# Another beginning, another pick of VectorE scores and of probability tiles in a two-branch attention kernel on one core

## The chip, the cores and the metric

One core of a Trainium2 chip runs the whole program. Its engines work side by side, each through its own queue in order: TensorE (PE; its weight loads are listed as PEld), VectorE (DVE), ScalarE (ACT), GpSimd (POOL) and SyncE (SP). An instruction may wait for semaphores that other engines or transfers raise; what stands behind it in its queue then waits too. The metric is the device time of one execution in microseconds, the median of several runs.

## The reference

Two attention branches over the same x (2048 x 512, 32 heads of 16), mixed by a gate for each row.

```python
x = A_x
g = sigmoid((x * gate_w).sum(-1, keepdims=True))
# branch A: 32 query heads, one key and one value head for all of them
q = (x @ wq).reshape(B, S, H, Dh).transpose(0, 2, 1, 3); k = x @ wk; v = x @ wv
p = softmax(einsum("bhqd,bkd->bhqk", q, k) * Dh ** -0.5)
a = einsum("bhqk,bkd->bhqd", p, v) ... @ wo
# branch B: 32 heads, each with its own keys and values
qkv = (x @ wqkv).reshape(B, S, 3, H, Dh) ...
b = softmax(q @ k.T * Dh ** -0.5) @ v ... @ wo
return g * a + (1 - g) * b
```

That is 2 x 32 x 2048 x 2048 exponentials, and two small matrix products around each.

## The kernel before

*Units of work.* The scores are computed with keys on the partitions and queries along the free axis. One *score* is a tile of 128 x 1024 (two heads, 512 queries each) in PSUM: eight matmuls of 32 columns by 512 (`products`, L576). There are 2048 scores, in pairs (a *quad* of two tiles `q`, `q+1`); 32 quads make a *phase*, four phases a pair of branch and head group; branch A and B alternate over four groups (`phases`, `quads`). A score becomes probabilities by one exp on ScalarE (L583), which writes a probability tile `prob0` to `prob5`. Some scores go to VectorE instead: TensorE writes them to a spare PSUM bank (`pair<-Q..`), and VectorE computes the exponential by a chain of seven passes (`chain`, L763 to L775) in tiles `vec`. The probabilities are multiplied with the values into a PSUM bank that gathers over the phase (`values`, L624), a quad at a time: in one piece of 512 columns, or in two halves of 256. TensorE takes four instructions for each of its f32 matmuls, so a full product of a quad is 32 instructions and two halves are 64; a score is 16.

*What surrounds it.* Query, key and value projections (L195) run through the other bank of `pair`, VectorE splits their result into a high and a low f16 half (L401, L404), and transfers lay the halves at the places where the score matmuls read them (`lay`, L359, issued by SP and POOL). After each phase the sums are normalised (`normalised`, L516 to L532) and multiplied by the output weights (`o_unit`).

*What sets the order.* Nothing is scheduled at run time. While the program is built, a planner (`_Plan`, `pe_step`) keeps a clock for each engine, with fixed costs (EXP 904 ns, SCORES 215, HALF 430 and so on), and writes out each engine's instructions in the order in which it believes they become possible. `score_time` says when the next score may go; until `limit` (the last exp's start plus SLACK) `pe_step` fills TensorE with value products (`value_job`), and with projection or output jobs or a VectorE score (`spare_job`). `pick` chooses the VectorE score: the last one left of the running phase, or, when the time left doesn't do for a chain, the last one of the next phase. For the next phase it asks first that the operands are laid (`laid`); for the running one it doesn't ask.

*The beginning* is written by hand up to the loop at the end of `_fast`: eight x tiles are turned by TensorE (L272; `x_in` and `x_unit`), scaled and split by ScalarE (L280) and VectorE (L285); the first query projection, the first half of the shared keys and values (`kv_products`, L300, and `kv_split`), the turn of the keys (`k_turn`, L332) and its copy (`k_put`, L335). x tile 7 and the second half of keys, values and gate (`kv_unit`, `gates`; z in L942 to L956) go through the planner as jobs.

*Probability tiles* are taken from a queue: the one that has been free longest (`free_probs.popleft()` in `score`).

## Time and profile before

| | |
|---|---|
| median of 3 runs | 1883.47 us (1883.21 to 1886.42) |
| profiled execution, its own time | 1883.59 us |
| its span, first to last instruction | 1881.8 us |
| mean TensorE clock granted | 0.990 |
| busy: PE / PEld / DVE / ACT / POOL | 94% / 45% / 65% / 96% / 20% |
| exps on ScalarE (L583) | 1942, busy 1787.0 us |
| chains on VectorE (first pass, L763) | 106 |

How to read the rows below. In a timeline row stand the start from the span's first instruction, the length, engine, line, operation, out<-in, shapes, the count of instructions that were merged, and in brackets the engine's idle time before and what ended it. In a row of stretches stand from:to, the length, then busy time and count, the clock granted to TensorE, the DMA share and GB/s. In a row of the chain of waits stand the start, the length and the work; "issue" is time in which the engine waited for nothing that the profile shows. A busy TensorE isn't TensorE at its peak, since matmuls are pipelined and their ends are modelled.

### The profile page before, as it was taken

The page shows a single profiled execution, that of the slowest core. Times are in us where ns is not written, and L with a number is a line of the kernel's source. Part 1 is how long each engine was busy: PE and PEld are TensorE (multiplying, and loading weights), DVE is VectorE, ACT ScalarE, POOL GpSimd, SP SyncE. Part 2 cuts the span into 40 slices and gives each one's busy share as a digit, 9 for nine tenths or more (in the row PEclk, how much of TensorE's full clock was granted, in tenths as well). Part 3 has the DMA queues.
Part 4 walks back from the last instruction along what each step waited for, and adds up shares of the span by engine and source line. Part 5 has one row for each costly group of instructions (what it writes and reads, how often), then busy time and mean ns, then how long its engine had stood idle before and what let it go on. Part 6 is the DMA issues. An engine that isn't in the chain of part 4 may idle for free.

```text
span 1881.8 us, 97974 instructions
## 1 busy us (share of the span) xinstructions
PE 1761.2 (94%) x45072; PEld 849.9 (45%) x45072; DVE 1217.6 (65%) x1380; ACT 1797.6 (96%) x1957; POOL 380.8 (20%) x569
## 2 busy tenths in 40 slices
PE   7999999999999999999999999999999999998994
PEld 5444444444444444444444444444444444444441
DVE  5267522969566565878558663797856856478983
ACT  4899999999999999999999999999999999999993
POOL 4302101232032111314021401231202310130000
PEclk9999999999999999999999999999999999999997
DMA  5121211223141141414133313241413213234011
GB/s 149 43 52 43 70 43 49 75 59 65 32 88 42 37 76 36 87 26 83 30 68 56 66 36 51 56 82 42 76 28 68 54 37 64 49 61 123 26 48 59
DMA packets 74067, 109.71 MB, mean 58 GB/s; under 512 B 20640, under 2 KB 29088, under 8 KB 73648
## 3 DMA queue, kind: packets, MB, share of 16 engines
q0 software_dynamic: 27808, 44.30, 14.0%
q1 hardware_dynamic: 43888, 56.41, 11.8%
q8 instruction: 355, 5.82, 1.3%
q10 hardware_dynamic: 1952, 2.66, 0.4%
q14 instruction: 64, 0.52, 0.1%
HBM read 14.75 MB, written 33.55 MB: 26 GB/s over the span
## 4 chain that ended last, share of the span: by engine, by line
ACT 67%; PE 16%; issue 12%; DVE 3%; DMA 1%; SPq 1%; POOL 0%; ACTq 0%; DVEq 0%; POOLq 0%
ACT prob L583 67%; PE pair L624 7%; PE sc L576 4%; PE pair L195 3%; DVE vec L775 1%; PE pt L272 1%; DMA K<-lokb 0%; SPq L516 0%; SPq L359 0%; DVE xT L470 0%; DVE sum L476 0%; PE pair L272 0%; DMA oT<-raw 0%; DMA vec<-in_A_x_dram 0%; PE pair L300 0%
## 5 line engine op out<-in xcount | busy, mean ns | idle before, releaser
L583 ACT ACTIVATE prob<-sc 128x1024 f32<-128x1024 f32 x1942 | 1787.0, 1077 | 23.9 <-PE sc L576 22.4
L624 PE MATMUL pair<-prob,vA 64*32 64x512 f32 (+1 forms) x8112 | 524.8, 577 | 0.1
L624 PE MATMUL pair<-prob,vB 64*32 64x512 f32 (+1 forms) x7984 | 517.4, 574 | 1.6 <-issue 1.4
L576 PE MATMUL sc<-Qb,K 64*32 64x512 f16 x7696 | 408.4, 382 | 44.7 <-ACT prob L583 36.2
L576 PE MATMUL sc<-Qa,kA 64*32 64x512 f16 x7840 | 407.7, 380 | 29.1 <-ACT prob L583 22.1
L576 PEld LDWEIGHTS <-K 64*32 64x32 f16 x8192 | 203.3, 90 | 434.0 <-issue 396.0
L576 PEld LDWEIGHTS <-kA 64*32 64x32 f16 x8192 | 202.7, 89 | 408.4 <-issue 366.9
L775 DVE SCALAR_TENSOR_TENSOR vec<-vec,vec 128x1024 f32<-128x1024 f32 x318 | 385.7, 1225 | 2.1
L763 DVE TENSOR_SCALAR vec<-pair 128x1024 int32<-128x1024 f32 x106 | 128.7, 1214 | 75.2 <-PE pair L576 74.9
L624 PEld LDWEIGHTS pair<-prob,vB 64*32 64x32 f32 x7984 | 156.5, 105 | 23.7 <-issue 4.2
L624 PEld LDWEIGHTS pair<-prob,vA 64*32 64x32 f32 x8112 | 155.2, 105 | 20.0 <-issue 2.0
L486 POOL DMA_DIRECT2D out_dram<-sum x48 | 59.4, 1240 | 384.6 <-DVE sum L476 384.6
L775 DVE SCALAR_TENSOR_TENSOR vec<-vec 128x1024 f32<-128x1024 f32 x106 | 128.8, 1215 | 0.9
L476 DVE TENSOR_SCALAR sum<-pair,gate_up 128x512 f32<-128x512 f32 x112 | 78.3, 738 | 75.1 <-PE pair L195 75.1
L523 DVE RECIPROCAL dT<-dT 128x256 f32<-128x256 f32 (+1 forms) x66 | 111.5, 1693 | 20.3 <-DMA dT<-raw 20.3
L359 POOL DMA_DIRECT2D Qa<-loqa x122 | 59.5, 495 | 294.2 <-DVE loqa L404 238.7
L359 POOL DMA_DIRECT2D Qb<-loqb x128 | 65.4, 519 | 236.2 <-PE sc L576 235.5
L401 DVE TENSOR_SCALAR hivb<-pair 128x1024 f16<-128x1024 f32 x8 | 9.8, 1224 | 122.4 <-PE pair L195 122.4
L677 DVE COPY raw<-pair 128x1024 f32<-128x1024 f32 x32 | 39.1, 1223 | 73.9 <-PE pair L624 73.7
L359 POOL DMA_DIRECT2D K<-hikb x64 | 33.3, 520 | 253.8 <-DVE hikb L401 253.8
L401 DVE TENSOR_SCALAR hikb<-pair 128x1024 f16<-128x1024 f32 x8 | 9.8, 1224 | 114.9 <-PE pair L195 114.9
L195 PE MATMUL pair<-w16ob,o 64*32 64x512 f16 x1536 | 64.4, 391 | 14.5 <-ACT o L529 6.8
(141 smaller groups left out, 1275.3 us busy)
## 6 DMA issues: line engine op xcount, KB each, us to landing
out_dram<-sum POOLq DMA_DIRECT2D x48, 512.0 KB, 5.9
dT<-raw SPq DMA_DIRECT2D x126, 64.0 KB, 2.1
vB<-vB SPq DMA_DIRECT2D x16, 384.0 KB, 4.0
Qb<-loqb POOLq DMA_DIRECT2D x128, 32.0 KB, 2.6
Qb<-hiqb SPq DMA_DIRECT2D x128, 32.0 KB, 2.5
out_dram<-sum SPq DMA_DIRECT2D x8, 512.0 KB, 3.7
xT<-out_dram SPq DMA_DIRECT2D x16, 256.0 KB, 6.9
oT<-raw SPq DMA_DIRECT2D x126, 32.0 KB, 2.9
```

The costliest lines, as they stand in the source:

```text
L195: nc.tensor.matmul(outs[n : n + COLS, i], lhs[i][rows(i), n : n + COLS], rhs[i][rows(i)], start=start, stop=stop)
L359: fns.append(lambda q=queues[(8 * p + n) % len(queues)], dst=dst, src=hilo[part][at]: q.dma_start(dst, src))
L401: nc.vector.tensor_scalar(hilo[0], pair[1], UP ** -1, None, op0=ALU.mult)
L476: nc.vector.tensor_scalar(state["sum"][:, e], pair[1][:, e], g, None, op0=ALU.mult)
L486: done = plan.on_pool([lambda: nc.gpsimd.dma_start(dst, state["sum"], accum_op=ALU.add)], t, 1300)
L523: nc.vector.reciprocal(d[:, c : c + cut], d[:, c : c + cut])
L576: nc.tensor.matmul(bank[a : a + COLS, hh], k[rows(hh), key : key + COLS], Q[src, gi, half, p][rows(hh), j * BLK : (j + 1) * BLK], start=Tr ...
L583: nc.scalar.activation(probs[u], sc, AF.Exp, scale=SCALE / (UP * UP))
L624: nc.tensor.matmul(pair[0][32 * k : 32 * k + 32, i, cols], v[rows(i)], probs[2 * m + k // 2][rows(i), hh, cols], start=first, stop=last)
L677: nc.vector.tensor_copy(state["raw"], full)
L763: nc.vector.tensor_scalar(tile("p").bitcast(I32), pair[1], SCALE / (UP * UP) / math.log(2) * 2.0 ** 23, None, op0=ALU.mult)
L775: nc.vector.scalar_tensor_tensor(p, m if i == 3 else p, VEC[i], m if i else w, op0=ALU.add, op1=ALU.mult)
```

## The change

Line numbers of the new kernel are higher: L576 is now L589, L583 is L602, L624 is L643, L195 is L205, L272 is L282, L332 is L345.

*The beginning.* Half of the first key and value products go ahead of the query products. ScalarE issues none of the query's transfers any more; SP and POOL take turns, high halves first. Tiles 2 and 3 of the first queries are laid after x tile 5. The key parts come ahead of the value parts in VectorE's first split, and the turned keys go through the spare bank. x tiles 6 and 7 are no longer turned ahead of the first exps and in planner's jobs, but in one piece right after the first two scores. The jobs of the second half of keys and values are reckoned shorter (160 instead of 330 ns), so that more of them fit between two scores.

On TensorE, where the first scores stand (pt4 and pt5 are banks for x tiles 4 and 5, vec6 and sum0 hold x tiles 6 and 7, sc0 to sc3 are the first scores). Before:

```order
L272 MATMUL pt4_670<-ident_85,vec4_107 64x128 x16
L332 MATMUL pair0_82<-ident16_86,sum1_111 128x128
...
L272 MATMUL pt5_698<-ident_85,vec5_108 64x128 x16
L272 MATMUL pair1_83<-ident_85,vec6_109 64x128 x16
L576 MATMUL sc0_739<-Qa000_621,kA_88 32x512
...
L576 MATMUL sc1_750<-Qa001_622,kA_88 32x512
...
L576 MATMUL sc2_761<-Qa000_621,kA_88 32x512
...
L272 MATMUL pair1_83<-ident_85,sum0_110 64x128 x4
```

Now:

```order
L282 MATMUL pt4_653<-ident_85,vec4_107 64x128 x16
L345 MATMUL pair1_83<-ident16_86,sum1_111 128x128
...
L282 MATMUL pt5_681<-ident_85,vec5_108 64x128 x16
L589 MATMUL sc0_716<-Qa000_621,kA_88 32x512
...
L589 MATMUL sc1_726<-Qa001_622,kA_88 32x512
...
L282 MATMUL pair0_82<-ident_85,sum0_110 64x128 x16
L282 MATMUL pair1_83<-ident_85,vec6_109 64x128 x16
L589 MATMUL sc2_776<-Qa000_621,kA_88 32x512
...
L589 MATMUL sc3_786<-Qa001_622,kA_88 32x512
```

x tile 6 has moved from ahead of the first score to behind the second, and x tile 7, which stood in four parts between the next scores, stands whole ahead of tile 6. The second half of the key and value products is done after the 20th score; before, it was done ahead of the 33rd, with its last 84 matmuls in two blocks there. The gate's activation on ScalarE stands after the 23rd exp instead of after the 32nd.

*VectorE scores.* `pick` asks for laid operands in both cases, and 96 scores go to VectorE instead of 106. On TensorE, at the start of the first phase of branch B's second group (scores from 768; Qb100 and Qb101 are query tiles, K10 and K11 their keys, a pair on the left is a bank for VectorE, a projection or the sums). Before:

```order
L576 MATMUL sc768_17155<-Qb100_14664,K10_13841 32x512
...
L576 MATMUL pair0_82<-Qb100_14664,K10_13841 32x512
...
L576 MATMUL sc769_17173<-Qb101_14665,K11_13842 32x512
...
L624 MATMUL pair1_83<-prob2_99,vA0_89 32x512 x4
...
L576 MATMUL sc772_17236<-Qb100_14664,K10_13841 32x512
...
L576 MATMUL pair1_83<-Qb101_14665,K11_13842 32x512
```

Now:

```order
L589 MATMUL sc768_17582<-Qb100_15373,K10_14521 32x512
...
L205 MATMUL pair0_82<-xT_84,w16kb10_9342 32x512
...
L589 MATMUL sc769_17608<-Qb101_15374,K11_14522 32x512
...
L643 MATMUL pair1_83<-prob1_98,vA1_90 32x512 x4
...
L589 MATMUL sc772_17709<-Qb100_15373,K10_14521 32x512
...
L643 MATMUL pair1_83<-prob3_100,vB0_91 32x256 x4
```

The two VectorE scores behind scores 768 and 772 are gone, here and in the same phase of the third and fourth group. The projection of the second half of the keys (w16kb10) stands there instead: it ended at score 762 before and ends at 776 now (1274 and 1280 in the third group, 1786 and 1800 in the fourth, whose phases start at 1280 and 1792). Value products of 256 columns have come in.

*The planner's numbers.* A start of an exp is reckoned 536 ns after its score instead of 456, SLACK is 368 instead of 404, with 36 ns more for full products of VectorE's probabilities alone. A model of TensorE's store of instructions is added (`takes`, `scant`; RATE, STORE, SCANT); with SCANT above STORE, `scant` always answers yes. The value products of 230 quads of ScalarE's tiles are written in halves instead of 35, and TensorE's instructions up to the end of the work grow from 90,147 to 96,227. A half-done quad on VectorE is finished first when its phase nears the end (`pressing`).

*Probability tiles.* For the first score of a quad the planner takes a free tile whose last writer ScalarE has already waited for, else the tile written last. On ScalarE, exps 7 to 10 before, with the semaphores they wait for:

```order
L583 ACTIVATE prob_97<-sc_828 128x1024 [waits PE_49,Activation_49]
L583 ACTIVATE prob_98<-sc_843 128x1024 [waits PE_49,Activation_49]
L583 ACTIVATE prob_99<-sc_871 128x1024 [waits PE_49,Activation_49]
L583 ACTIVATE prob_100<-sc_886 128x1024 [waits PE_49,Activation_49]
...
```

And exps 10 to 14 now:

```order
L602 ACTIVATE prob_102<-sc_903 128x1024 [waits PE_49,Activation_49]
L602 ACTIVATE prob_99<-sc_931 128x1024 [waits PE_49]
L602 ACTIVATE prob_100<-sc_978 128x1024 [waits PE_49,Activation_49]
L602 ACTIVATE prob_101<-sc_997 128x1024 [waits PE_49]
L602 ACTIVATE prob_102<-sc_1043 128x1024 [waits PE_49,Activation_49]
```

Of 1942 exps before, all but the first six waited for an earlier instruction of ScalarE itself; of 1952 now, 974 do.

```diff
-EXP, EXP_ENDS, EXP_AFTER = 904, 1136, 456
+EXP, EXP_ENDS, EXP_AFTER = 904, 1136, 536
-SLACK = 404
+SLACK, TIGHT = 368, 404
+RATE, STORE, SCANT = 0.062, 200, 201
...
+    def takes(self, n):
+
+        self.store = min(self.store + (self.pe - self.seen) * RATE, STORE) - n
+        self.seen = self.pe
+
+    def scant(self):
+        return min(self.store + (self.pe - self.seen) * RATE, STORE) < SCANT
...
     def score(u):
...
-        probs[u] = free_probs.popleft()
+        known = [n for n, tile in enumerate(free_probs) if wrote.get(id(tile), 0) <= wrote["seen"]]
+        n = known[0] if known and not u % 2 else max(range(len(free_probs)), key=lambda n: wrote.get(id(free_probs[n]), 0))
+        probs[u] = free_probs[n]
+        del free_probs[n]
+        wrote["n"] += 1
+        wrote["seen"] = max(wrote["seen"], wrote.get(id(probs[u]), 0))
+        wrote[id(probs[u])] = wrote["n"]
...
-        wide = BLK if n == 0 and room >= 2 * HALF else BLK // 2
+        wide = BLK if n == 0 and plan.scant() and room + TIGHT - SLACK >= 2 * HALF else BLK // 2
...
         if left_in(ph) * EXP > need:
             found = [m for m in range(at[0] + 2, 32 * ph + 32) if m not in vector]
         elif ph < LASTS:
-            found = [m for m in range(32 * ph + 32, 32 * ph + 64) if m not in vector]
             ph += 1
-            if max(laid(ph, NT - 1, phases[ph][2] + e) for e in range(2)) + 3000 > now:
-                return None
+            found = [m for m in range(32 * ph, 32 * ph + 32) if m not in vector]
         else:
             return None
+        if max(laid(ph, NT - 1, phases[ph][2] + e) for e in range(2)) + 3000 > now:
+            return None
...
-            if job and now + job[1] <= (limit if get is mine or not part[0] else min(limit, t + LATE)):
+            to = limit + TIGHT - SLACK if get is mine and job and job[1] > HALF else limit
+            if part[0] and get is not mine and plan.scant():
+                to = min(to, t + LATE)
+            if job and now + job[1] <= to:
...
-        jobs = [(lambda i=i, n=n: kv_products(1, i, pair[1], STEPS[n : n + 6]), 330) for i in range(4) for n in range(0, 24, 6)]
-        return _Unit(jobs, finish, lambda now: turned_x[0] == 1, lambda: 1000)
+        jobs = [(lambda i=i, n=n: kv_products(1, i, pair[1], STEPS[n : n + 6]), 160) for i in range(4) for n in range(0, 24, 6)]
+        return _Unit(jobs, finish, lambda now: turned_x[0] == 2, lambda: 1000)
...
+    for i in range(2):
+        kv_products(0, i, pv, STEPS)
     for n in range(len(STEPS)):
         product(weights["a", 0, "q"], 0, n, spare)
-    for i in range(4):
+    for i in range(2, 4):
         kv_products(0, i, pv, STEPS)
...
-    both = (nc.sync, nc.scalar, nc.gpsimd)
-    for p in range(4):
-        for fn in lay(hilo, to[p], p, (0, 1, 0, 1), both if p < 2 else (nc.sync, nc.gpsimd)):
+
+    def first_q(p):
+        for fn in lay(hilo, to[p], p, (0, 1, 0, 1), (nc.sync, nc.gpsimd)):
             fn()
         ready["q", "a", 0, 0, p] = 0.0 if p < 2 else 8000.0
-    kn, take, halve = kv_split(0, pv)
-    take()
+
+    first_q(0)
+    first_q(1)
+    kn, take, halve, k_top = kv_split(0, pv)
+    take(value=False)
     halve()
+    take(nc.gpsimd, key=False)
     x_in(4, more())
+    for i in range(8):
+        k_turn(kn, spare, i)
+    k_put(0, spare)
     x_lo(4, as_x(banks[-1]))
-    for i in range(8):
-        k_turn(kn, pv, i)
-    k_put(0, pv)
     x_in(5, more())
     x_lo(5, as_x(banks[-1]))
-    x_in(6, spare)
-    x_lo(6, as_x(spare))
...
+    while not at[0]:
+        pe_step()
+    free["pv"] = free["spare"] = math.inf
+    for k, which in ((7, "pv"), (6, "spare")):
+        bank = as_x(pair[which == "spare"])
+        for c in range(NK):
+            for w in range(2):
+                x_turn(k, bank, c, w)
+        x_free(k)
...
+        one = plan.vec(lambda k=k, bank=bank: x_hi(k, bank, nc.vector), 1130, 0.5 + which.count("sp"), plan.pe + TO_VEC)
+        plan.vec(lambda k=k, bank=bank: x_lo(k, bank), 1130, 0.5 + which.count("sp"), 0.0, (one,), then)
```

More of the change, by code (lines that the diff above doesn't have):

```diff
@@ L352, in lay @@
     def lay(hilo, to, p, parts, queues):
-        n, fns = 0, []
-        for hh in range(2):
+        fns = []
+        for n, part in sorted(enumerate(parts * 2), key=lambda x: x[1]):
+            hh = n // 4
             at = slice((2 * p + hh) * DH, (2 * p + hh + 1) * DH)
-            for part in parts:
-                dst = to[hh * ROWS + n % 4 * DH :][:DH].rearrange("d (a q) -> d a q", a=2)
-                fns.append(lambda q=queues[(8 * p + n) % len(queues)], dst=dst, src=hilo[part][at]: q.dma_start(dst, src))
-                n += 1
+            dst = to[hh * ROWS + n % 4 * DH :][:DH].rearrange("d (a q) -> d a q", a=2)
+            fns.append(lambda q=queues[len(fns) % len(queues)], dst=dst, src=hilo[part][at]: q.dma_start(dst, src))
         return fns
@@ L722, in vector_job @@
     def vector_job(now):
-        if chained() > WORK + (EXTRA if half_vec else 0):
+        if chained() > WORK + (EXTRA if half_vec else 0) and not pressing():
             return None
@@ L742, in job @@
             held[1] += 1
+            plan.takes(16)
             products(u, pair[1])
@@ L843, in run @@
             unit.jobs.popleft()
+            plan.takes(16)
             fn()
@@ L861, in pe_step @@
             score(u)
+            plan.takes(16)
             plan.exp(now)
@@ L896, in _fast @@
     turned_x = [0]
-    def x_unit(k):
-        def finish(t):
-            def then(end):
-                free["spare"] = end + FROM_VEC
-                turned_x[0] += 1
-                plan.vec(lambda: x_top(k), 1130, 4, end, due=end + 60000)
-            x_free(k)
-            a = plan.vec(lambda: x_hi(k, as_x(pair[1]), nc.vector), 1130, 1, t + TO_VEC)
-            plan.vec(lambda: x_lo(k, as_x(pair[1])), 1130, 1, 0.0, (a,), then)
-        jobs = [(lambda c=c, w=w: x_turn(k, as_x(pair[1]), c, w), 215) for c in range(NK) for w in range(2)]
-        return _Unit(jobs, finish, lambda now: True, lambda: 100 * k)
     def kv_unit():
         def finish(t):
-            kn, take, halve = kv_split(1, pair[1])
+            kn, take, halve, k_top = kv_split(1, pair[1])
             def turn_k():
@@ L922, in finish @@
                     plan.vec(lambda: k_put(1, pair[1]), 600, 1, t + TO_VEC, (), then)
-                jobs = [(lambda i=i: [k_turn(kn, pair[1], 4 * i + e) for e in range(4)], 330) for i in range(2)]
+                jobs = [(lambda i=i: [k_turn(kn, pair[1], 4 * i + e) for e in range(4)], 215) for i in range(2)]
                 units.append(_Unit(jobs, finish, lambda now: True, lambda: 1000))
```

51 lines of the change are left out of this document (35 added, 16 removed).

## The prediction, made before the changed kernel was run

> **What bounds the kernel.** I read the page first, then ScalarE's busy time by stage, then its timeline and the chain of waits at the places where it stands idle.
>
> ```profile
> span 1881.8 us, 97974 instructions
> PE 1761.2 (94%) x45072; PEld 849.9 (45%) x45072; DVE 1217.6 (65%) x1380; ACT 1797.6 (96%) x1957; POOL 380.8 (20%) x569
> ACT 67%; PE 16%; issue 12%; DVE 3%; DMA 1%; SPq 1%; POOL 0%; ACTq 0%; DVEq 0%; POOLq 0%
> L583 ACT ACTIVATE prob<-sc 128x1024 f32<-128x1024 f32 x1942 | 1787.0, 1077 | 23.9 <-PE sc L576 22.4
> ```
>
> ScalarE's exps (L583) carry the end: they are 67% of the chain. The next view is ScalarE in ten stretches from the first exp to the last (length, busy time, instructions, TensorE clock, DMA share, GB/s).
>
> ```profile
> 34.90:70.40 35.50, 29.98 (x34) 1.00 0.28 74
> 70.40:266.00 195.60, 195.10 (x213) 1.00 0.18 45
> 266.00:310.00 44.00, 39.90 (x43) 1.00 0.27 63
> 310.00:720.00 410.00, 408.25 (x446) 1.00 0.28 57
> 720.00:734.00 14.00, 9.70 (x11) 0.88 0.36 77
> 734.00:1175.00 441.00, 439.98 (x479) 1.00 0.29 55
> 1175.00:1185.00 10.00, 5.75 (x7) 0.83 0.47 100
> 1185.00:1628.00 443.00, 439.87 (x480) 1.00 0.28 53
> 1628.00:1638.00 10.00, 5.99 (x7) 0.83 0.45 99
> 1638.00:1851.10 213.10, 212.67 (x232) 1.00 0.24 60
> ```
>
> Length less busy is idle time: 5.5 in the first stretch, 4.3, 4.25 and 4.0 in the three short ones (12.6 together), and 0.5 + 4.1 + 1.75 + 1.0 + 3.1 + 0.4 = 10.9 in the rest. That is all that a better order can win between first and last exp: 29.0 us. Everything else there is the exps' own time, and the next rows say what one costs.
>
> ```profile
> 34.89 5.60 ACT L583 ACTIVATE prob<-sc 128x1024 f32<-128x1024 f32 x6
> 46.34 5.62 ACT L583 ACTIVATE prob<-sc 128x1024 f32<-128x1024 f32 x6
> 542.70 55.13 ACT L583 ACTIVATE prob<-sc 128x1024 f32<-128x1024 f32 x60
> ```
>
> These are ScalarE's timeline: six exps, six exps, sixty exps in a row. By the third, with a last exp of 1.077 us, one exp follows another after (55.13 - 1.077) / 59 = 0.916 us. [...]
>
> **The change, part by part.**
>
> *Ten scores go from VectorE back to ScalarE.* 106 VectorE scores become 96, 1942 exps become 1952. ScalarE pays 10 x 0.916 = +9.2 us, on the path. VectorE is freed of ten chains and TensorE of nothing; VectorE is at 65%, so I count that at zero.
>
> *VectorE scores wait for laid operands.* The three short stretches are one event, once in each of the last three groups. Their rows at the first (timeline, with idle time and releaser in brackets):
>
> ```profile
> 721.05 1.22 DVE L401 TENSOR_SCALAR hikb<-pair 128x1024 f16<-128x1024 f32 x1 [22.48 <-PE pair L195]
> 725.84 0.40 PE L576 MATMUL pair<-Qb,K 64*32 64x512 f16 x4 [1.53 <-DMA K<-lokb]
> 727.57 0.61 PE L576 MATMUL pair<-Qb,K 64*32 64x512 f16 x4 [1.33 <-DMA K<-lokb]
> 728.72 1.02 ACT L583 ACTIVATE prob<-sc 128x1024 f32<-128x1024 f32 x1 [3.28 <-PE sc L576]
> 730.76 1.94 ACT L583 ACTIVATE prob<-sc 128x1024 f32<-128x1024 f32 x2 [1.02 <-PE sc L576]
> ```
>
> A VectorE score (pair<-Qb,K) stands in TensorE's queue ahead of keys that are still in flight; TensorE takes its queue in order, the next scores for ScalarE stand behind it, and ScalarE idles 3.28 + 1.02. The new order has no VectorE score in that phase at all. What is late next: the same key half is needed by ScalarE's own scores only 32 scores into the phase, 29 us, and in the new order its projection ends at the latest 8 scores into it, so 22 us remain against the 6.5 us from the start of the split (721.05) to the last wait's end (727.57) above. I take the whole idle time, -12.5. The bounds are the direct waits alone, 3 x (1.53 + 1.33) = -8.6, and -12.6.
>
> *The beginning.* Rows of the timeline up to the first exps, and of the place where the second half of the shared keys is turned:
>
> ```profile
> 15.03 1.02 ACT L280 ACTIVATE xT<-pt 128x1024 f16<-128x1024 f32 x1 [0.72 <-PE pt L272]
> 16.11 5.63 PE L195 MATMUL pair<-xT,w16qa 64*32 64x512 f16 x192 [1.11 <-ACT xT L280]
> 21.67 2.33 PE L300 MATMUL pair<-wkv,xT 64*128 64x33 f16 x158
> 25.67 0.60 PE L300 MATMUL pair<-wkv,xT 64*128 64x33 f16 x34 [1.67 <-issue]
> 26.20 2.68 PE L272 MATMUL pt<-ident,vec 128*64 128x128 f32 x32
> 28.81 1.03 PE L332 MATMUL pair<-ident,sum 128*128 128x128 f16 x8
> 29.19 1.02 ACT L280 ACTIVATE xT<-pt 128x1024 f16<-128x1024 f32 x1 [13.13 <-DMA Qa<-hiqa]
> 32.01 1.91 PE L272 MATMUL pair<-ident,vec 128*64 128x128 f32 x32
> 33.28 1.23 DVE L285 SCALAR_TENSOR_TENSOR xT<-pt,xT 128x1024 f16<-128x1024 f32 x1 [1.21 <-ACT xT L280]
> 33.97 1.02 ACT L280 ACTIVATE xT<-pair 128x1024 f16<-128x1024 f32 x1 [0.72 <-PE pair L272]
> 69.94 0.21 ACT L945 ACTIVATE z<-z 128x16 f32<-128x16 f32 x1 [5.16 <-DVE z L942]
> 70.42 2.85 ACT L583 ACTIVATE prob<-sc 128x1024 f32<-128x1024 f32 x3 [0.27 <-PE sc L576]
> ```
>
> The page adds what one piece of a laid query costs, its issue on GpSimd's queue (mean ns) and its flight (us):
>
> ```profile
> L359 POOL DMA_DIRECT2D Qb<-loqb x128 | 65.4, 519 | 236.2 <-PE sc L576 235.5 <-issue 0.2
> Qb<-loqb POOLq DMA_DIRECT2D x128, 32.0 KB, 2.6
> ```
>
> Half of the key and value products (96 of 192, at 2.33 / 158 = 14.7 ns: 1.4 us) now stand ahead of the query products, where TensorE idled 1.11. So the query products end at 15.0 + 1.4 + 5.63 = 22.0 instead of 21.74, and the other half at 23.4. The 1.67 us in which TensorE waited to issue falls on the same count of instructions, so I leave it in: 25.1 instead of 26.27. From there TensorE runs x tile 4 (2.68), the key turn (1.03) and x tile 5 (2.68) to 31.5; ScalarE's copy (1.02) and VectorE's low half (1.23) follow to 33.8. ScalarE's queue now holds none of the query transfers that held its copy for 13.13, and x tile 6 no longer stands ahead of the first score. The query pieces of the first two tiles go by two queues instead of three, eight on each: 8 x 0.52 + 2.6 = 6.8 us after VectorE's high half at 23.3 is 30.1, before the first score. The first exp starts near 32.5, the second near 34.3.
>
> Then x tiles 7 and 6 are turned in one piece, 2 x (1.91 to 2.68), and ScalarE waits: third score at 34.2 + 4.3 = 38.5, its exp at 38.9, two microseconds behind the old order, in which the third of the six exps started at 34.89 + 2 x 0.905 = 36.7. The gain comes later. In the old order the key and value products of the second half crept along, and ScalarE stood 5.16 us at the gate activation and its successor began at 70.42. In the new order they end after the 20th score, so the same 33rd exp starts at 38.9 + 30 x 0.916 + 0.21 = 66.6. VectorE must have both x tiles split by the 9th exp at 44.4: four passes of 1.23 and two reductions between them, taken as long, end 7.4 us after 36.3 (the end of x tile 7's turn), at 43.7. That is close. Sum: -3.8. Bounds: -5.5 if the 1.67 goes too; +1.4 if the 5.16 stays.
>
> *Narrow value products.* 195 more pairs of probability tiles are multiplied in two halves of 256 columns instead of one of 512. The chain of waits prices both:
>
> ```profile
> 270.05 0.86 PE pair L624 x16
> 273.14 0.43 PE pair L624 x16
> 273.79 0.86 PE pair L624 x32
> 275.17 1.44 issue
> ```
>
> A full one takes 0.86, a half 0.43, two halves 0.86. Cost zero in TensorE's time, as long as instructions arrive; each split adds 32 of them, 6,080 in all. The last row is that cover gone: TensorE stood 1.44 us with nothing to wait for but its instructions, after a run of halves. Taken at zero, because the densest runs of the two orders are alike, 64 and 66 instructions for one exp over sixteen exps; upper bound +7.2, five such waits; lower bound zero.
>
> *Choice of probability tiles.* 974 exps instead of 1936 wait for an earlier exp of ScalarE itself. The first of the timeline rows above has six exps without that wait, the second six with it: 5.60 and 5.62. Taken at zero; bounds zero and the third rival. *New constants* (a later start after a score, less slack) only shape the order; the remaining 10.9 us of idle time may be reshuffled. I take it unchanged, with -6 to +6, a little over half.
>
> Sum: +9.2 - 12.5 - 3.8 = -7.1 us. The profiled execution took 1883.59 (span 1881.8 and 1.8 around it), 0.1 above the median of 1883.47. So 1883.5 - 7.1 = 1876.4.
>
> **Rivals.**
>
> *The idle time only moves* (no change). The key wait gives its lower bound, 8.6, the beginning gives nothing because VectorE is late with x tile 6: -8.6 + 9.2 = +0.6, 1884.1. For it: every stall above stood in an order whose planner believed in none. Against it: the two mechanisms are cut at their roots, and only the beginning is close.
>
> *Instructions run short* (slower). Place: the two stretches where key projections and half-width values alternate, at scores 771 to 782 and their like a thousand scores on, and the 5 pairs of exps in which key and value products are now packed three times as densely. Each wait there costs 1.44 to 1.67 us as in the rows at 275.17 and 25.67. Five of them eat the gain, since 7.1 / 1.44 = 4.9; with twelve the time is 1876.4 + 17.3 = 1893.7. Against it: these two are the only ones over a microsecond in the list of TensorE's waits, and the count of instructions grows by 7%.
>
> [...]
>
> *Exps run faster without their own wait* (much faster). If the 0.905 us between starts in the first row, (5.60 - 1.077) / 5, were kept up, 1952 x 0.011 = 21 us more would go: 1855. Against it: the six exps with the wait have the same pace, so it is the pace of a start after a pause.
>
> **How the numbers follow.** 0.2%, 3.8 us, is about what a measurement of this kernel can tell from no change. The forecast, with what lies round it (1866 to 1879.7), gets 0.65; faster exps 0.04; idle time that only moves 0.16; short instructions 0.15. So faster 0.69, same 0.16, slower 0.15. The range: below, the sum of the lower bounds beside the reshuffling, 1883.5 + 9.2 - 12.6 - 5.5 - 6 = 1868.6, and 2 more for terms that I don't see; above, the moved idle time with four instruction waits, 1884.1 + 5.8 = 1890. That leaves out most of the faster exps and the worse part of short instructions, some 2 in 10 with the tails.
>
> **What would show it.** Right: no VectorE matmul waits for K at the start of the last three groups' B phases, and ScalarE's idle time there is under 0.5 each; the gate activation waits under 1 us; a pause of about 4 us after the second exp; exps still 0.916 apart, 1952 of them; last exp to end still 30.7 (from 1851.1 to 1881.8). Wrong: "issue" waits of TensorE by the dozen; ScalarE idle over 8 us in the first 70; more than 17 us of idle time outside the places named; another pace of the exps.

## The result: slower, and the profile after

The changed kernel takes 1901.24 us (median of 4 runs, 1897.03 to 1901.61) against 1883.53 beside it: a ratio of 1.0086 (95% interval 1.0068 to 1.0103). That is 16 us slower by the ratio, where 7 faster was forecast.

The page of the kernel after (span, engines, the chain by engine, the exps):

```profile
span 1899.8 us, 103065 instructions
PE 1770.6 (93%) x48112; PEld 897.0 (47%) x48112; DVE 1153.4 (61%) x1311; ACT 1806.4 (95%) x1966; POOL 385.4 (20%) x574
ACT 73%; PE 12%; issue 8%; DMA 2%; DVE 2%; SPq 1%; POOL 1%; ACTq 0%; DVEq 0%; POOLq 0%
L602 ACT ACTIVATE prob<-sc 128x1024 f32<-128x1024 f32 x1952 | 1797.0, 1123 | 37.7 <-PE sc L589 37.1
```

ScalarE still carries the end. The span grew by 18.0: ten more exps, 10.0 of busy time (1787.0 to 1797.0); more time between first and last exp that isn't an exp, 8.5 (29.2 to 37.7); the end after the last exp, 0.9 (30.7 to 31.7); and 1.5 less ahead of the first exp (34.89 to 33.41). The same ten stretches of ScalarE as in the prediction, the last one to the new last exp:

```profile
34.90:70.40 35.50, 28.73 (x32) 0.95 0.30 80
70.40:266.00 195.60, 192.99 (x211) 1.00 0.21 49
266.00:310.00 44.00, 44.00 (x49) 1.00 0.20 51
310.00:720.00 410.00, 402.77 (x438) 1.00 0.27 56
720.00:734.00 14.00, 13.01 (x15) 1.00 0.03 8
734.00:1175.00 441.00, 432.44 (x472) 0.99 0.29 57
1175.00:1185.00 10.00, 10.00 (x12) 1.00 0.01 3
1185.00:1628.00 443.00, 433.73 (x472) 1.00 0.27 54
1628.00:1638.00 10.00, 9.92 (x12) 1.00 0.35 82
1638.00:1868.20 230.20, 228.42 (x249) 1.00 0.24 60
```

The three short stretches had 12.6 us of idle time; now they have 1.1. The key waits are gone. But the long stretches, which had 10.9 together, have 29.5 (2.6, 7.2, 8.6, 9.3, 1.8, to which the third adds nothing). TensorE's waits tell by what (in all, times, longest). After:

```profile
PE pair L589 <- DVE sum L488: 6.1, 3, 4.0
PE pair L643 <- issue: 5.5, 8, 0.9
PE pair L205 <- issue: 4.3, 4, 1.3
PE pair L643 <- DVE raw L697: 3.7, 6, 0.7
PE pair L310 <- DMA wkv<-wkv: 3.4, 1, 3.4
PE sc L589 <- issue: 2.2, 5, 0.9
PE pair L439 <- issue: 1.2, 2, 0.7
```

Before, the rows of the same kinds:

```profile
PE pair L576 <- DMA K<-lokb: 8.8, 6, 1.6
PE pair L300 <- issue: 1.7, 1, 1.7
PE pair L576 <- DVE sum L476: 1.7, 1, 1.7
PE pair L624 <- issue: 1.4, 1, 1.4
PE sc L576 <- issue: 0.9, 3, 0.5
```

Waits for nothing but instructions were 4 us and are 13.2. Waits of a VectorE score for the bank that an output sum still holds were 1.7 and are 6.1. One of each in the timeline after, with what surrounds it:

```profile
559.75 0.63 PE L643 MATMUL pair<-prob,vA 64*32 64x256 f32 x16
560.18 0.40 PE L205 MATMUL pair<-w16ob,o 64*32 64x512 f16 x3
561.80 0.40 PE L205 MATMUL pair<-w16ob,o 64*32 64x512 f16 x5 [1.22 <-issue]
562.49 1.02 ACT L602 ACTIVATE prob<-sc 128x1024 f32<-128x1024 f32 x1 [1.17 <-PE sc L589]
...
879.24 1.48 POOL L221 TENSOR_SCALAR wqb<-wqb 128x512 f32<-128x512 f32 x1 [2.34 <-DMA wqb<-in_B_wqkv_dram]
880.79 0.61 POOL L222 CAST w16qb<-wqb 128x512 f16<-128x512 f32 x1
881.43 0.69 DVE L214 TENSOR_REDUCE stats<-w16qb 128x1 f32<-128x512 f16 x1 [6.47 <-POOL w16qb L222]
882.04 1.40 DVE L488 TENSOR_SCALAR sum<-pair,gate_up 128x512 f32<-128x512 f32 x2
883.49 0.73 PE L589 MATMUL pair<-Qb,K 64*32 64x512 f16 x8 [4.02 <-DVE sum L488]
884.75 1.02 ACT L602 ACTIVATE prob<-sc 128x1024 f32<-128x1024 f32 x1 [4.07 <-PE sc L589]
```

Above, TensorE stops in the middle of a projection's eight matmuls. Below, VectorE stands 6.47 us at a reduction that only collects a new weight's maximum: the weight is late on GpSimd. Behind it in VectorE's queue is the output sum, behind that the bank, behind that the VectorE score and in TensorE's queue the next score for ScalarE.

Put together from the trace, each idle stretch of ScalarE between exps laid to the longest wait of TensorE (over 0.15 us) ahead of the score that ended it (us; "operands": keys or queries in flight; "busy": TensorE had no such wait). The 5.2 us in which ScalarE waits at the gate's activation with the old beginning aren't in it:

```
kernel        issue        VectorE  operands  busy   sum
before        2.6 (x4)       2.0       9.5     9.0   23.1
after        15.6 (x19)     13.7       0       8.4   37.7
1st run      10.3 (x15)      7.6       1.5     9.1   28.4
2nd run      10.8 (x11)      7.7      26.9     8.5   53.9
4th run       7.1 (x11)      8.4       2.3     8.3   26.1
6th run       4.2 (x7)       4.1       2.3     7.3   17.9
8th run       6.1 (x8)       1.5       5.9     1.9   15.3
9th run       9.8 (x15)      2.3      10.0     8.6   30.6
11th run     12.6 (x14)      8.1       5.9     2.6   29.2
13th run      5.0 (x7)      15.4       0       9.5   29.9
```

From before to after, waits for instructions add 13.0 and waits for VectorE 11.7; the keys give back 9.5. Of the 13.7 behind VectorE, 5.5 are output sums, 4.9 copied sums (`raw`), 1.9 the turn of the second half of the keys and 1.5 chains. In the eighth and the eleventh run 4.7 of the "operands" are the pause in which x tiles 7 and 6 are turned, which stands under "busy" in the kernel after.

### The profile page after: what moved, and what is told of

It reads as the page before. It is cut to its first block, busy times and chain, and to the rows that moved or that the text cites. A ratio compares the mean times of both kernels' runs of the same rounds, so it can differ in the third digit from the quotient of the medians.

```text
span 1899.8 us, 103065 instructions
## 1 busy us (share of the span) xinstructions
PE 1770.6 (93%) x48112; PEld 897.0 (47%) x48112; DVE 1153.4 (61%) x1311; ACT 1806.4 (95%) x1966; POOL 385.4 (20%) x574
## 3 DMA queue, kind: packets, MB, share of 16 engines
q8 instruction: 378, 6.19, 1.3%
q10 hardware_dynamic: 1792, 2.49, 0.4%
## 4 chain that ended last, share of the span: by engine, by line
ACT 73%; PE 12%; issue 8%; DMA 2%; DVE 2%; SPq 1%; POOL 1%; ACTq 0%; DVEq 0%; POOLq 0%
ACT prob L602 73%; PE pair L643 5%; PE sc L589 3%; PE pair L205 2%; SPq L372 1%; DMA wvb<-in_B_wqkv_dram 1%; DMA wqb<-in_B_wqkv_dram 1%; SPq L528 0%; DVE vec L791 0%; DMA wkv<-wkv 0%; POOL wvb L221 0%; DMA prob<-in_gate_w_dram 0%; DVE xT L482 0%; PE pair L282 0%; PE pair L439 0%
## 5 line engine op out<-in xcount | busy, mean ns | idle before, releaser
L602 ACT ACTIVATE prob<-sc 128x1024 f32<-128x1024 f32 x1952 | 1797.0, 1123 | 37.7 <-PE sc L589 37.1
L643 PE MATMUL pair<-prob,vA 64*32 64x512 f32 (+1 forms) x9760 | 551.3, 506 | 6.9 <-issue 3.8
L643 PE MATMUL pair<-prob,vB 64*32 64x512 f32 (+1 forms) x9536 | 542.3, 511 | 2.4 <-issue 1.8
L589 PE MATMUL sc<-Qb,K 64*32 64x512 f16 x7760 | 411.6, 382 | 46.1 <-ACT prob L602 36.5
L589 PE MATMUL sc<-Qa,kA 64*32 64x512 f16 x7856 | 414.1, 381 | 24.4 <-ACT prob L602 16.0
L589 PEld LDWEIGHTS <-K 64*32 64x32 f16 x8192 | 204.3, 89 | 413.6 <-issue 365.4
L589 PEld LDWEIGHTS <-kA 64*32 64x32 f16 x8192 | 203.3, 89 | 376.5 <-issue 327.7
L803 DVE SCALAR_TENSOR_TENSOR vec<-vec,vec 128x1024 f32<-128x1024 f32 x288 | 350.0, 1228 | 2.1
L643 PEld LDWEIGHTS pair<-prob,vA 64*32 64x32 f32 x9760 | 187.4, 105 | 36.7 <-issue 9.3
L643 PEld LDWEIGHTS pair<-prob,vB 64*32 64x32 f32 x9536 | 185.4, 105 | 27.3 <-issue 3.3
L791 DVE TENSOR_SCALAR vec<-pair 128x1024 int32<-128x1024 f32 x96 | 116.9, 1218 | 51.2 <-PE pair L589 51.0
L803 DVE SCALAR_TENSOR_TENSOR vec<-vec 128x1024 f32<-128x1024 f32 x96 | 117.4, 1223 | 1.2
L372 POOL DMA_DIRECT2D Qa<-hiqa x64 | 32.6, 515 | 398.8 <-DVE hiqa L413 377.6
L205 PE MATMUL pair<-w16ob,o 64*32 64x512 f16 x1536 | 72.2, 392 | 17.7 <-ACT o L541 6.7
L205 PEld LDWEIGHTS <-o 64*32 64x32 f16 x3072 | 51.7, 93 | 51.0 <-issue 13.5
```

Of the source, the lines that this page charges most:

```text
L205: nc.tensor.matmul(outs[n : n + COLS, i], lhs[i][rows(i), n : n + COLS], rhs[i][rows(i)], start=start, stop=stop)
L372: fns.append(lambda q=queues[len(fns) % len(queues)], dst=dst, src=hilo[part][at]: q.dma_start(dst, src))
L589: nc.tensor.matmul(bank[a : a + COLS, hh], k[rows(hh), key : key + COLS], Q[src, gi, half, p][rows(hh), j * BLK : (j + 1) * BLK], start=Tr ...
L602: nc.scalar.activation(probs[u], sc, AF.Exp, scale=SCALE / (UP * UP))
L643: nc.tensor.matmul(pair[0][32 * k : 32 * k + 32, i, cols], v[rows(i)], probs[2 * m + k // 2][rows(i), hh, cols], start=first, stop=last)
L791: nc.vector.tensor_scalar(tile("p").bitcast(I32), pair[1], SCALE / (UP * UP) / math.log(2) * 2.0 ** 23, None, op0=ALU.mult)
```

## The experiments

All ratios are to the kernel before, run beside it; its own median lay between 1883.5 and 1887.4 us, so a difference of 2 or 3 us between medians of separate measurements says nothing by itself. Edits are made to the kernel named in each expectation. The runs are numbered in the order in which they were made, which is not that of this section.

**Which constant makes the halves.** The first run sets the lead from a score to its exp back in the kernel after, the second raises it in the kernel before:

```diff
-EXP, EXP_ENDS, EXP_AFTER = 904, 1136, 536
+EXP, EXP_ENDS, EXP_AFTER = 904, 1136, 456
```

> The kernel after with one constant set back: the planner again reckons 456 ns, not 536, from a finished score to its exp. That alone makes the planner split as few value products as before: 164 halves instead of 556, 89,955 TensorE instructions instead of 96,227, and 1950 exps. The rest of the change stays. Theory of the instructions: TensorE's waits with nothing to wait for but its instructions go from 13.2 us to about 4, ScalarE's idle time behind them from 15.6 to about 3, and the time falls by some 12 us, to 1887 to 1891. Rival, that the waits come from the new places of the VectorE scores and of the beginning, whatever the number of instructions: it stays within 4 us of 1901.

Measured 1887.8, ratio 1.0014 (1.0005 to 1.0023): 13 us faster than the kernel after, as the theory had it. But its reason holds only in part: waits for instructions fell from 15.6 to 10.3, not to 3; the rest came from VectorE's side.

> The kernel before with that constant alone: 536 instead of 456 ns. 494 halves instead of 176, 95,235 TensorE instructions instead of 90,147, 1944 exps and 104 VectorE scores. Theory of the instructions: more than ten waits of about a microsecond for instructions, ScalarE's idle time behind them over 10 us instead of 2.6, and a time of 1892 to 1898. Rival: two more exps are all that is paid, 1884 to 1887.

Measured 1917.2, 1.0168 (1.0154 to 1.0182), far more than either theory. Waits for instructions are as foreseen, 10.8 us in 11. The surprise is in the key waits, 26.9 of idle time: with the longer lead, and a pick that doesn't ask, VectorE scores stand still further ahead of their keys (9.1, 8.9 and 8.8 us at the three places). In the change the guard hides what the constant would do.

**Probability tiles**, the third run in the kernel after, the tenth in the kernel before:

```diff
-        known = [n for n, tile in enumerate(free_probs) ...
...
+        probs[u] = free_probs.popleft()
```

> The kernel after, but each exp writes the probability tile that has been free longest, as before. The order of all instructions is the same to the last row; nearly every exp again waits for an earlier exp of ScalarE, 1950 or so instead of 974. The prediction counted this part at zero: within 2 us of 1901. Rival from the gaps between exps after the change (mean 909.9 and 913.8 ns on even and odd scores, against 912.1 and 917.2 before): the choice gains 2.8 ns for each exp, 4 to 8 us, and this kernel takes 1905 to 1909.

Measured 1904.0, 1.0107 (1.0092 to 1.0123): 3 to 4 us above the kernel after, with intervals that overlap.

> The kernel before with the new choice of probability tiles and nothing else; the order of instructions is the same. About half of the exps lose their wait for an earlier exp. By the gaps between exps in the kernels after and of the third experiment, ScalarE's pace gains 2.6 us over the program: 1881 to 1883 where the kernel before takes 1884 to 1885. Rival, the prediction's zero: within 1 us of the kernel before.

Measured 1882.2, 0.9987 (0.9977 to 0.9996): a gain of 2.5 us, for the same order of instructions. The choice helps a little.

**The guard alone** (fourth run), and another way to the same end (fifth), both in the kernel before:

```diff
         else:
             return None
+        if max(laid(ph, NT - 1, phases[ph][2] + e) for e in range(2)) + 3000 > now:
+            return None
```

> The kernel before, with laid operands asked for in both cases of the pick and nothing else changed. 98 VectorE scores, 1950 exps, 166 halves. The prediction's terms: 8 more exps, +7.3, and the key waits gone, -12.5, so 1878.3, with ScalarE idle for under 0.5 us at each of the three places around 728, 1180 and 1633. Rival, that a wait of the same size comes up somewhere else: 1884 to 1891.

Measured 1894.2, 1.0044 (1.0030 to 1.0057): the guard by itself costs 8 us. ScalarE's idle time behind keys fell from 9.5 to 2.3, behind VectorE it rose from 2.0 to 8.4 and behind instructions from 2.6 to 7.1; 8 exps came on top. VectorE's own waits in this kernel and in the kernel after:

```profile
DVE stats L204 <- POOL w16qb L212: 21.8, 4, 6.6
```

```profile
DVE stats L214 <- POOL w16qb L222: 16.4, 3, 6.5
```

The kernel before has this wait too (6.4 us in 3), with hardly anyone behind it.

```diff
+        q = phases[ph][2]
+        found = [m for m in found if max(laid(ph, quads[m][1], q + e) for e in range(2)) + 3000 <= now]
-        return 2 * found[-1]
+        return 2 * found[-1] if found else None
```

> The kernel before; only the pick is changed, in another way than in the kernel after: of the quads that it may take it drops those whose operands are not laid, and takes the last that is left. In the three phases with the key waits it takes the 16th quad, whose keys are in the first half, in place of the 32nd. 106 VectorE scores and 1942 exps stay. If the key waits are the whole cost there, ScalarE's 12.5 us of idle time around 728, 1180 and 1633 go and nothing is paid: 1871 to 1875. Rival, that the idle time comes back at another place, as after the guard: 1880 or more.

Measured 1873.6, 0.9931 (0.9915 to 0.9947), a gain of 12 us with nothing paid. ScalarE is busy all of 720 to 734, 1175 to 1185 and 1628 to 1638; the first of these:

```profile
720.00:734.00 14.00, 14.00 (x16) 1.00 0.29 59
```

The prediction's price of the key waits was right; only the way in which the change removes them costs more.

**The late weight maximum**, sixth run with the guard alone, eleventh in the kernel after:

```diff
-            plan.vec(lambda: absmax(f"w{part}_{src}", gi, pair[0][:, 0]), 590, 4, at + 500, due=at + 20000)
+            plan.vec(lambda: absmax(f"w{part}_{src}", gi, pair[0][:, 0]), 590, 4, at + 12000, due=at + 40000)
```

> The kernel before with the guard, as in the fourth experiment, and one more edit: the reduction on VectorE that reads a new weight's maximum is planned 12 us after the weight's split on GpSimd, not 0.5. In the fourth experiment VectorE stood 21.8 us in four waits at that reduction for GpSimd, the output sums stood behind it, the bank for the next VectorE score behind these, and ScalarE idled 6.6 us. Theory: these waits go, and with 1948 instead of 1950 exps the time falls by 4 to 8 us, to 1886 to 1890. Rival, that the output sums are late for their own reasons: within 2 us of 1894.

Measured 1880.8, 0.9974 (0.9963 to 0.9985): 13 us less than with the guard alone, more than expected, since waits for instructions became fewer as well (7 instead of 11, in an order that shifted a little).

> The kernel after with the late reduction alone: a new weight's maximum is read on VectorE 12 us after the split, not 0.5. 1952 exps, 556 halves and 96,227 instructions as in the kernel after. In the kernel after VectorE stands 16.4 us at that reduction, and ScalarE idles 5.5 us behind output sums. Theory: 4 to 8 us go, 1893 to 1897. If the sixth experiment's 13 us come back here, 1888. Rival: within 2 us of 1901.

Measured 1891.1, 1.0033 (1.0021 to 1.0045), 10 us less than the kernel after. No idle time behind output sums is left, of 5.5.

**The beginning alone** (seventh run: the beginning's code of the kernel after, the rest of the planner as before):

> The beginning of the kernel after with all else as before: the old pick, the oldest probability tile, 456 ns from score to exp, slack 404. 106 VectorE scores, 1942 exps, 182 halves. The prediction's term for this part is -3.8. In the profile of the third experiment, where TensorE's clock is granted in full through the beginning, the 33rd exp starts at 67.45 (prediction 66.6); in that of the kernel after, with the clock at 0.5 in the turn of x tiles 7 and 6, at 70.94 (before: 70.42). So -3 with the full clock and about zero without it, a median of 1880 to 1884. Rival: the beginning costs time of its own, over 1886.

Measured 1887.6, 1.0008 (0.9999 to 1.0018): no gain, a loss of 0 to 3 us. Part of the reason is seen in the rows of the kernel after, two of its timeline for each engine and two stretches of TensorE (length, busy, count, granted clock, DMA):

```profile
35.03 3.12 PE L282 MATMUL pair<-ident,sum 128*64 128x128 f32 x32
37.93 2.48 PE L282 MATMUL pair<-ident,vec 128*64 128x128 f32 x32
40.82 18.18 ACT L602 ACTIVATE prob<-sc 128x1024 f32<-128x1024 f32 x19 [4.65 <-PE sc L589]
60.87 1.02 ACT L602 ACTIVATE prob<-sc 128x1024 f32<-128x1024 f32 x1 [1.87 <-PE sc L589]
```

```profile
20.00:24.00 4.00, 4.00 (x120) 0.75 0.00 0
36.00:38.00 2.00, 2.00 (x24) 0.50 0.34 74
```

And of the third run, which has the same order:

```profile
34.59 1.97 PE L282 MATMUL pair<-ident,sum 128*64 128x128 f32 x32
36.38 1.92 PE L282 MATMUL pair<-ident,vec 128*64 128x128 f32 x32
38.71 1.02 ACT L596 ACTIVATE prob<-sc 128x1024 f32<-128x1024 f32 x1 [2.98 <-PE sc L589]
```

```profile
20.00:24.00 4.00, 4.00 (x163) 1.00 0.00 0
36.00:38.00 2.00, 2.00 (x42) 1.00 0.15 34
```

With the clock at half from 35.65 to 39.07, the two x tiles take 5.4 instead of 3.7 us from start to end. Of eight profiles with the new beginning seven have these dips; their 33rd exp starts between 70.66 and 72.90 (after 70.94), that of the third run at 67.45. In the eight profiles with the old beginning it starts between 69.20 and 70.42, and between 69.20 and 69.97 in the five of them without a dip. So the new beginning gains about 2 us where the clock is granted in full, which one profile shows, and nothing where it isn't.

The seventh run's loss isn't the clock alone. In its profile the 33rd exp comes 2.5 us later than before (72.90), and the old pick puts a VectorE score ahead of its keys at a place where the kernel before had none:

```profile
PE pair L589 <- DMA K<-lokb: 11.6, 7, 5.5
```

The 5.5 us end at 285.8, and ScalarE idles 5.98 behind them; at the three key waits that the kernel before has too, it idles 0.9 to 1.3 us less. So this run prices the beginning together with a key wait that the guard keeps out of the kernel after.

**Instructions by themselves**, ninth run:

```diff
-            values(m, slice(n, n + wide))
+            if wide == BLK and m % 5 == 2:
+                values(m, slice(0, BLK // 2))
+                values(m, slice(BLK // 2, BLK))
+            else:
+                values(m, slice(n, n + wide))
```

> The kernel before, order and all, but of every fifth full value product (m % 5 == 2) the two halves are multiplied one right behind the other, in the same place and for the same TensorE time. 187 more products in halves, 96,131 TensorE instructions, within 100 of the kernel after; 1942 exps, 106 VectorE scores. Nothing else moves, so this prices the instructions by themselves. Theory of the instructions: ScalarE's idle time behind waits for instructions grows from 2.6 us to 6 to 15, and the time is 1888 to 1897. Rival, that the waits of the kernel after come from the places of its work alone: within 2 us of the kernel before.

Measured 1893.6, 1.0045 (1.0028 to 1.0061): 9 us for instructions that do nothing new. Idle time behind them rose from 2.6 to 9.8. Its halves stand one right behind the other, other than in the kernel after, so it prices the instructions and not those places. TensorE's waits of this kind:

```profile
PE pair L427 <- issue: 4.6, 7, 1.1
PE pair L624 <- issue: 3.9, 4, 1.7
PE pair L300 <- issue: 1.9, 2, 1.7
PE sc L576 <- issue: 1.8, 4, 0.8
```

Why at these places? The trace has each fetch of 16 KB of instructions (queue q8, 378 packets and 6.19 MB in the kernel after) with its start. Counted from the first, every one of the 17 waits over 0.25 us in the kernel after stands at the same place of a block of 256, give or take one. Eight of them (us; "lasted": from the entry into the block before to the stop; "fetch": its start after that entry, with a median of 0.75 over all blocks; KB of other transfers between entry and fetch):

```
wait ends   wait   lasted   fetch     in flight
  130.12    0.68    4.69     2.94     660 KB, SP's queue
  431.87    1.34    5.44     3.77     508 KB, GpSimd's
  561.80    1.22    4.63     3.66     512 KB, GpSimd's
 1123.93    0.73    2.40     0.70     none
 1153.57    0.88    4.75     3.40     512 KB, GpSimd's
 1345.39    0.85    5.79     4.37     710 KB, GpSimd's
 1498.78    0.84    4.92     3.50     510 KB, GpSimd's
 1571.35    0.94    5.68     4.28     512 KB, GpSimd's, 146 SP's
```

TensorE goes on 2.2 to 3.0 us after the fetch's start. Most blocks here weren't dense; the fetch came late. In eleven of the 17 an output sum was on its way to memory in GpSimd's queue, in three a load of SP's. Late fetches aren't new: in the kernel before 30 of 352 start more than 2.2 us after the entry, and two of them stop TensorE; in the kernel after it is 21 of 375, and 14 do. What differs is the length of a block, in the median 5.07 us before and 4.79 after. In the ninth run seven of 16 such waits stand behind half a megabyte in flight; the other nine end blocks of 1.8 to 3.5 us with next to nothing in flight. The thirteenth run takes the output sums away:

```diff
-                    done = plan.on_pool([lambda: nc.gpsimd.dma_start(dst, state["sum"], accum_op=ALU.add)], t, 1300)
+                    done = plan.on_pool([lambda: nc.gpsimd.dma_start(dst[:, :, :64], state["sum"][:, :, :64], accum_op=ALU.add)], t, 1300)
```

> The kernel after, in the same order to the last row, but each output sum that GpSimd's queue adds to the result in memory carries 64 of 512 columns, 64 KB instead of 512: seven eighths of these sums are left out of the result. In the kernel after each of the 17 waits for instructions stands at a multiple of 256 instructions from the one before, and 9 of them behind such a transfer: TensorE's instruction fetch starts 2.5 to 4.4 us after TensorE has entered the block before, against a median of 0.75. Theory: those nine go, ScalarE's idle time behind waits for instructions falls from 15.6 us to 6 to 9, and the time to 1892 to 1896. Rival, that blocks of 256 instructions are just used up too fast, whatever else is in flight: 15 or more such waits stay and the time stays above 1898.

(The list above has eleven behind such a transfer; the expectation's nine were miscounted.) Measured 1889.3, 1.0013 (1.0001 to 1.0026), 12 us less than the kernel after in medians, 14 by the ratios and 10 in the profiles, with the same instructions in the same order. Seven waits are left, 5.0 us of idle time:

```profile
PE pair L439 <- issue: 1.6, 3, 0.8
PE pair L643 <- issue: 1.4, 2, 0.8
PE pair L205 <- issue: 1.0, 1, 1.0
PE sc L589 <- issue: 0.5, 1, 0.5
```

Two of them are behind loads in SP's queue, one behind half a megabyte in both queues, four behind nothing. So two things meet: a fetch that starts 2.3 to 4.4 us after the entry while a bulk transfer is in flight, and blocks shortened by halves that no longer outlast it. The first is shown by this run, the second by the ninth and by the lengths above.

**Put together**, the eighth, fourteenth and twelfth run:

> The kernel after with three edits: 456 ns from score to exp, the pick of the fifth experiment, the late reduction of the sixth. 106 VectorE scores, 1942 exps, 186 halves, 90,307 instructions. From the first experiment's 1887.8: 8 exps less, -7.3; waits for output sums gone, up to -4.2; fewer dense stretches of TensorE instructions (27 instead of 45 stretches of four exps with over 256), up to -4. 1872 to 1880.

Measured 1867.1, 0.9897 (0.9881 to 0.9914): faster than both kernels by more than expected.

```diff
-                    done = plan.on_pool([lambda: nc.gpsimd.dma_start(dst, state["sum"], accum_op=ALU.add)], t, 1300)
+                    done = plan.on_pool([lambda e=e: nc.gpsimd.dma_start(dst[:, e], state["sum"][:, e], accum_op=ALU.add) for e in range(2)], t, 650)
```

> The eighth kernel, in the same order on TensorE, with each of GpSimd's output transfers issued as two of 256 KB, one behind the other. If a fetch can slip in between the two, the waits behind such a transfer (2 of the 8 in the eighth kernel's profile, at 447 and 1452) get shorter, at most 1 to 2 us in all: 1865 to 1867. If the second piece is queued at once and the fetch waits for both, or the added issue on GpSimd (48 times 1.2 us) delays another wait: 1867 to 1871.

Measured 1865.3, 0.9879 (0.9858 to 0.9900), the fastest, though not told apart from the eighth. Two waits of the old kind are still there, at other places: splitting the transfer isn't shown to free the fetch. At the one that ends at 789 us, 510 KB of GpSimd's queue, so both pieces, moved before the fetch began, 4.2 us after the entry. (The eighth profile had a third such wait, at 1683, that the expectation doesn't count.)

> The kernel before with the pick of the fifth experiment, the late reduction and the new choice of probability tiles; the old beginning, 456 ns. 1942 exps, 106 VectorE scores, 174 halves. Against the eighth experiment it differs most by the beginning: there the 33rd exp started at 71.5 us in the profile, with the old beginning at 69.4 to 70.4 in three. From the fifth experiment's 1873.6: output sums -3.5, tile choice 0 to -3, so 1866 to 1871; if the new beginning is worth the prediction's 3.8, this one stays above 1870.

Measured 1874.2, 0.9944 (0.9930 to 0.9958), above the expectation and no better than the fifth run alone. One new wait of TensorE for a VectorE chain (4.7 us of ScalarE's time) eats what the late maximum gives. It says little on the beginning.

## Why the prediction was wrong

- *Ten more exps, +9.2*: right, 10.0.
- *Key waits, -12.5*: right at the place (12.6 to 1.1) and as a price (the fifth run's 12). Wrong in the step "What is late next". It looked at ScalarE's scores and the key projection and left out where the VectorE scores go instead: next to output products, whose sums VectorE clears late because it waits for a weight's maximum. With the exps the guard is +8, not -3 to -5.
- *The beginning, -3.8*: measured 0 to +3, with the seventh run's new key wait in it. What failed is the size of "x tiles 7 and 6 are turned in one piece, 2 x (1.91 to 2.68)", taken at 4.3: 5.4 in the kernel after, at a clock of 0.5. Two steps were missing: the key and value products ahead of the query products wait 3.4 for their swapped weights, and the key turn makes the score behind it wait 1.87 at 60.87 (0.39 in the third run). There the 33rd exp comes 0.5 later than before, not 3.8 earlier. With the clock granted in full the times came out near the forecast, third exp at 38.71 (38.9), 33rd at 67.45 (66.6), but in part by luck: the query products end at 24.82 there, 2.8 later than the forecast's 22.0, because the wait for the weights is in that run too (3.0), and the turns of x tile 4, keys and x tile 5 made up for it, 1.97, 0.62 and 1.97 in place of 2.68, 1.03 and 2.68. The forecast's lengths come from the kernel before at a time when its own clock had dipped:

```profile
28.00:32.00 4.00, 4.00 (x50) 0.66 0.54 120
```

- *Narrow value products, 0*: this step failed most. "The densest runs of the two orders are alike" was true and beside the point: most waits (14 of 17) come in blocks that aren't the densest, where the fetch started 2.3 to 4.4 us after the entry. Measured 9.0 by themselves. The rival "instructions run short" was right in kind and near in number (19 waits in place of its 12, and shorter ones), mostly wrong in place. The reading of the wait before at 276.61 (the 1.44 from 275.17), "after a run of halves", didn't ask what was in flight: it was 654 KB in SP's queue, with the fetch 2.5 us after the entry. Of the two long waits before only the one at 25.67 ends a dense block, of 1.8 us, with nothing else in flight.
- *New constants, 0*: the constant of 536 is what makes the halves (556 to 164 without it); 13 us. In the profiles ScalarE's idle time behind instructions fell by 5.3 with it, and behind VectorE by 6.1. Calling it one that "only shapes the order" separated the cause from its effect.
- *Probability tiles, 0*: a gain of 2.5; between zero and the rival's 21, close to zero.
- What was to show it wrong did: "issue" waits by the dozen, and more than 17 us of idle time outside the places named (29.5). ScalarE's idle time in the first 70, about 7.2 us, stayed under the 8.

The parts don't add up singly: the guard costs 8 and the constant 33 alone, and both with the rest only 16, since the guard stops what the longer lead does to the key waits. Not tried: the kernel after's waits for the copied sums (`raw`, 4.9 us of ScalarE's idle time).

## What to carry to other kernels

When an edit moves work away from a wait, follow it to its new place and read what that place's queues wait for, bookkeeping instructions included: a reduction that nobody needed soon held a bank that everybody needed (16.4 us of VectorE's waits, 5.5 of ScalarE's idle time in the kernel after). Instructions are a resource with a supply: at each one that an edit adds, ask how long a block of 256 lasts (a median of 4.79 us in the kernel after) and which bulk transfers run at the same time (14 of its 17 waits had one in flight), not only how dense the densest stretch is. And lengths read from the first 40 us hold only for the clock that was granted there (two x tiles took 5.4 us with a dip to 0.5, 3.7 at 1.00): read it beside them.

## What the runs showed of the hardware

- In the kernel after, TensorE's instruction fetch starts a median 0.75 us after a block's entry, but 2.3 to 4.4 us after it at the 14 waits with 0.45 to 1.1 MB in flight in GpSimd's or SP's queue, and TensorE went on 2.2 to 3.0 us after its start. With GpSimd's output sums cut to 64 KB (thirteenth run) the waits fell from 17 to 7.
- The granted clock fell to 0.5 in the first 40 us in seven of eight profiles with the new beginning (its mean over 14 to 44 us is 0.89 in each), but not in the third run's (1.00), and with the old beginning in three of eight profiles (0.94 in each). In the kernels before and after each of these dips lasts 3.41 us. The first in the kernel after (18.6 to 22.0) follows a pause of TensorE of 3.38; but before the dip at 35.65 TensorE's longest stretch without a matmul is 1.51 us, counted from the end of the first dip, and before the one at 27.29 in the kernel before it is 1.67, counted from its first matmul. The same order has 0.50 at 36 to 38 us in one execution and 1.00 in another. What sets a dip off isn't shown.
- An exp without a wait for an earlier exp was hardly faster: in the tenth run half of them lost it, and the program gained 2.5 us, 1.3 ns for each of all its exps.
